# Eight copies of a pair's turned selection as one step on one engine, load issues planned at 1.4, and a new set of ranks

## The chip, the cores and the metric

The kernel runs on 1 core of one Trainium2 chip. The time is the device time of one execution in microseconds (us); "time before" is the median of 3 runs. Five engines work side by side, each through its own list of instructions in order: PE (matrix products), ACT (activation functions and copies), DVE (vector work), POOL (masks, casts and some DMA issues) and SP (most DMA issues).

## The reference: what is computed

Attention with a selection of key chunks comes first, for 4 batches of 8 heads with 768 positions of 64 values; a gated feed-forward layer over the 3072 tokens follows.

```python
k_min = np.min(k_chunks, axis=3)          # chunks of 32 keys, 24 chunks
k_max = np.max(k_chunks, axis=3)
ub = np.sum(np.maximum(q * k_min, q * k_max), axis=-1)   # a bound per query and chunk
ub = np.where(causal, ub, -1e9)
top_chunks = np.argsort(ub, axis=-1)[..., -6:]           # each query keeps 6 chunks
scores = np.where(sel & causal_by_position, scale * (q @ k.T), -1e9)
attn = softmax(scores); attn_out = attn @ v
x = attn_out as 3072 tokens x 512;  xn = x / rms * rms_g
out = (silu(xn @ w_gate) * (xn @ w_val)) @ w_out         # 512 -> 1536 -> 512
```

## The kernel before, in words

**Units of work.** The heads are taken in pairs: 16 pairs, four to a batch. For each pair `prep` (L465) loads q and k (step names `qload`, `kload`, L491, on SP), turns them by PE (`qT`, `kT`, L501), copies them out of PSUM (`qE`, `kE`), reduces the chunks to minima and maxima (`kmn`, `kmx`, DVE), computes the bounds on PE (`ub`, L588), copies and turns them (`ubE`, `up`), finds the sixth largest (`max`, L629) and writes the selection into a tile `selq` (`sel`, L636 and L640). PE turns that (`selT`, L651) into a PSUM tile `st`, and eight copies of 32 x 192 elements (`selC`, L661, executed in the helper `evict` at L295 on ACT and L299 on DVE) bring it into the rows of the query tile `qs` that add the selection to the scores. One copy goes with each of the two heads (`hl`) and each of four quarters of the queries (`g`). `scores` (L694) then multiplies (`sc`, L719), exponentiates (`exp`, ACT, L736, tile `pt`), for batches 1 to 3 masks the diagonal on POOL (`mask`, L742), multiplies by v (`av`, L755) and divides (`xb`, DVE, L770 and L771). Pair 3 alone is done in two halves of the queries (`PARTS`, L243), so it has the places `s3.0` and `s3.3`; all others go whole.

**The feed-forward layer.** When all four pairs of a batch are done, `norm` (L783) scales the rows, half a batch at a time (`sq`, `eps`, `root`, `xs`; a turn by PE for batch 0, by DMA for the others), and `ffn` (L863) runs 12 blocks of `gate` (L883, four matmuls of 384 columns), `tanh` (ACT, L890), `tg` (DVE, L896), `val` (L904) and `hh` (DVE, L912), and then three output tiles of twelve matmuls (`po`, L924), each copied (`poE`) and stored (`out`, L939). 48 idle-time matmuls (`busy`, L342, rank 1000 and more) on zeros run when PE has nothing else at the start.

**What sets the order.** Nothing waits for a scheduler on the chip. All steps are added to a planner (`Order`, L79), which plays through time with a cost for each step and engine, and emits the instructions in the order in which its steps start. An engine that is free in the plan takes the ready step with the smallest rank (L126 to L154); where a step has costs for two engines, the first one to be free with nothing of smaller rank takes it. A rank is the place of the pair or half batch (`TIMES`: `a` for prep, `l` for loads, `s` for scores, `n` for norm, `f` for the feed-forward layer, `w` for weights) plus the number of the step's kind for batch 0 or the later batches (`RANK`), plus a pace. The planner also hands out the buffers: the 8 PSUM banks are shared by all kinds of tile (`ps=8`, L233), a bank going to the next tile when the plan says that its last user is done. In the program the real waits for buffers and data then hold whatever the plan assumed.

The plan's costs of a copy of n elements are `0.065 + n * 0.00083` on ACT (L281) and `0.07 + n * 0.00104` on DVE (L284). The steps around the change are:

```python
ld = [add(w + "load", "SP", 1.1, rank(lr, b, w + "load"), load, opens=[nat[w]], load=n * 550)] * 2
fin.append(add("selC", "", {"DVE": dve(nq / 2), "ACT": act(nq)},
               rank(at, b, "selC", hl, "step"), sel_out, [sT], opens=[c.set], uses=[st]))
need = list(c.sel) + c_qz + ...      # every sc step waits in the plan for all steps of c.sel
```

Here `nq` is 192, so the plan counts 0.224 us for a copy on ACT and 0.170 on DVE, and takes the eight for independent of each other.

Of the kernel before, what the change touches and what calls it, by code (L numbers as in the profile page):

```python
# [11 lines left out]
ACT = mybir.ActivationFunctionType  # L12
# [12 lines left out]

RANK = (
    dict(
        av=68.81, dif=27.84, eps=227.72, exp=-53.17, kC=174.37, kE=-146.3, kT=-410.53,
        kload=-41.08, kmn=-9.51, kmx=106.52, max=-184.96, qC=69.13, qE=207.98, qT=-151.24,
        qload=-40.04, relu=-83.35, root=-346.12, sc=-47.1, sel=-150.06, selC=272.89,  # L30
        selT=-45.75, sq=136.63, tp=-15.96, tpE=-44.6, ub=-307.31, ubE=23.65, ubm=-192.71,
        up=-160.23, vload=-327.49, xb=278.11, xs=-341.07,
    ),
    dict(
        av=-40.18, dif=78.51, eps=-121.68, exp=5.8, gate=-52.28, hh=-172.1, kC=-37.64,
        kE=163.43, kT=-18.13, kload=69.85, kmn=172.23, kmx=-38.93, mask=-59.31, max=121.45,
        out=-40.26, po=26.47, poE=28.63, qC=177.4, qE=15.98, qT=16.85, qload=40.35, relu=1.22,
        root=-157.61, sc=-29.47, sel=120.96, selC=24.49, selT=-332.65, sq=322.32, tanh=156.94,
        tg=27.97, ub=-2.65, ubE=-289.61, ubm=194.29, up=17.47, val=-42.44, vload=48.52,
        xT=-304.79, xb=-39.13, xs=-25.77,  # L40
    ),
)

TIMES = {
# [15 lines left out]
}  # L60


# [139 lines left out]
def kernel(  # L202
# [13 lines left out]
    B, H, S, D = q.shape  # L216
    assert (P, D) == (128, 64) and S == 768
    CH = 32
# [10 lines left out]
    G = 4  # L229
# [22 lines left out]
    def add(name, engs, occ, rank, *a, **kw):  # L252
        return order.add(name, engs, occ, rank if isinstance(rank, dict) else {"": rank}, *a, **kw)

    def rank(place, b, kind, n=0, pace=None):
        r = {place: 1.0, f"{kind}.{min(b, 1)}": 1.0}
        if n:
            r[pace] = float(n)
        return r
# [14 lines left out]
    def tile_of(b, shape, dtype, name):  # L274
        pool = ps if b.kind == "ps" else sb
        b.tile = pool.tile(shape, dtype, name=name, tag=f"{b.kind}{b.slot}")
        return b.tile


    def act(n):  # L280
        return 0.065 + n * 0.00083  # L281

    def dve(n):
        return 0.07 + n * 0.00104  # L284
# [42 lines left out]
    def make_ident(e):  # L327
# [7 lines left out]
        out=first[:], in_=ident_f[:, 0:1], func=ACT.Exp), [c_id])  # L335
# [69 lines left out]
    def make_tri(e):  # L405
# [10 lines left out]
        out=gains[:], in_=moe_rms_g.rearrange("(o n) -> o n", o=1).to_broadcast([P, DM])),  # L416
        load=140000)
# [14 lines left out]
    for part in range(2):  # L432
# [6 lines left out]
                load=1000000) for part in range(2)]  # L439
# [7 lines left out]
    def make_pair(p):  # L447
        c = Pair()
        c.p, (c.b, c.pr) = p, divmod(p, NP)
        c.h0 = 2 * c.pr  # L450
        c.set, c.ku, c.v = Buf("set"), Buf("ku"), Buf("vext")
        c.ke, c.dif = {}, {}
        return c
# [11 lines left out]
    def prep(c, i0, nb, at, lr):  # L465

        p, b, h0 = c.p, c.b, c.h0
# [3 lines left out]
        nat, big = {}, {}  # L471
        done = {}
        for w, src in (("k", k), ("q", q)):
            nat[w], big[w] = Buf("nat"), Buf("qt")

            def load(e, w=w, src=src, r0=0, rn=nb):
                if nat[w].tile is None:
                    tile_of(nat[w], [P, NT, 2, D], FP32, w + "nat")
                t = nat[w].tile
                for hl in range(2):  # L480
                    eng = nc.scalar if p == 0 and hl else nc.sync
                    eng.dma_start(out=t[:, r0:r0 + rn, hl, :],
                                  in_=src[b, h0 + hl, (i0 + r0) * P:(i0 + r0 + rn) * P].rearrange(
                                      "(t p) d -> p t d", p=P))

            if p == 0:
                ld = [add(w + "load", "SP", 0.2, -200 + 2 * (w == "q") + r0 / 3,
                          lambda e, load=load, r0=r0: load(e, r0=r0, rn=3), opens=[nat[w]],
                          load=3 * P * 550) for r0 in range(0, nb, 3)]
            else:  # L490
                ld = [add(w + "load", "SP", 1.1, rank(lr, b, w + "load"), load, opens=[nat[w]],  # L491
                          load=n * 550)] * 2

            evs = []
            for j0 in range(0, nb, 3):
                bank = Buf("ps", "prep")

                def turn(e, w=w, j0=j0, bank=bank):
                    t = tile_of(bank, [P, 3 * P], FP32, "p" + w)
                    for j in range(3):  # L500
                        nc.tensor.transpose(  # L501
                            t[:, j * P:(j + 1) * P],
                            nat[w].tile[:, j0 + j].rearrange("p h d -> p (h d)"), ident_f[:])

                tr = add(w + "T", "PE", 0.33, rank(at, b, w + "T", j0, "step"), turn, [ld[j0 // 3], c_id],
                         opens=[bank], uses=[nat[w]])

                def out_(e, w=w, j0=j0, bank=bank):
                    if big[w].tile is None:
                        tile_of(big[w], [P, S], FP32, w + "t")  # L510
                    evict(e, big[w].tile[:, j0 * P:(j0 + 3) * P], bank.tile[:])

                evs.append(add(w + "E", "", {"ACT": act(384), "DVE": dve(384)},
                               rank(at, b, w + "E", j0, "step"), out_, [tr],
                               opens=[big[w]], uses=[bank]))
            done[w] = evs
# [16 lines left out]
        step = 3 if p == 0 else nb  # L533
        for x0 in range(0, nb, step):
# [7 lines left out]
                    uses=[big["k"]])]  # L542

        def diff(e):
# [5 lines left out]
                 uses=[mx, c.ku], port=True)  # L550
# [4 lines left out]
        for w, dst in (("k", KE), ("q", QS)):  # L555
            for hl in range(2):
                rows = slice(hl * D, (hl + 1) * D)

                def cast(e, w=w, dst=dst, hl=hl, rows=rows):
# [4 lines left out]
                                 uses=[big[w]]))  # L564
# [4 lines left out]
        def relu(e):  # L569
# [5 lines left out]
                 uses=[big["q"]], port=True)  # L575


        nq = n // G
        ub = [Buf("ps", "prep") for _ in range(2)]
        ubs = Buf("ubs")  # L580

        def bounds(e):
            t = [tile_of(x, [P, nq], FP32, "ub") for x in ub]
            for m, src in ((0, big["q"].tile), (1, rel.tile)):
                for g in range(G):
# [9 lines left out]
                 uses=[c.ku, big["q"], rel])  # L595
        ue = []
        for h in range(2):
            def ub_out(e, h=h):
                if ubs.tile is None:
# [5 lines left out]
                          uses=[ub[h]]))  # L605
        up, ubm, m8 = Buf("ps", "prep"), Buf("ubm"), Buf("small")
# [9 lines left out]
        def causal(e):  # L616
# [6 lines left out]
                   opens=[ubm], uses=[up])  # L623
# [8 lines left out]
        sq = Buf("selq")  # L632

        def pick(e):
# [10 lines left out]
                 opens=[sq], uses=[m8, ubm], port=True)  # L645
        st = Buf("ps", "prep")
# [6 lines left out]
                    ident_b[:])  # L653

        sT = add("selT", "PE", NU * 0.057, rank(at, b, "selT"), sel_turn, [pk, c_idb], opens=[st], uses=[sq])
        fin = []
        for hl in range(2):
            for g in range(G):
                def sel_out(e, hl=hl, g=g):
                    rows = slice((1 - hl) * D, (1 - hl) * D + CH)  # L660
                    evict(e, QS[c.set.slot][hl][rows, g * nq:(g + 1) * nq],  # L661
                          st.tile[g * CH:(g + 1) * CH, hl * nq:(hl + 1) * nq])

                fin.append(add("selC", "", {"DVE": dve(nq / 2), "ACT": act(nq)},
                               rank(at, b, "selC", hl, "step"), sel_out, [sT],
                               opens=[c.set], uses=[st]))
        c.sel = fin
        return fin

# [273 lines left out]
    for p in range(NPAIRS):  # L943
        c, b = make_pair(p), p // NP
# [42 lines left out]
```

## Time and profile before

| what | us |
|---|---|
| median of 3 runs (331.98 to 332.43) | 332.0 |
| the profiled execution's own time | 334.32 |
| its span, first to last instruction | 332.6 |
| PE busy in the span | 316.3 (95%) |
| DVE busy | 249.3 (75%) |
| ACT busy | 210.4 (63%) |
| POOL busy | 118.5 (36%) |
| granted TensorE clock, mean | 0.993 |

The profile is of one execution. An engine's busy time is the time in which it runs instructions of its own; a wait is the idle time just before an instruction, put down to the work that ended last before it. The ends of matmuls are modelled, so PE's busy time is an upper figure of its work. "PE gp L883 <- ACT qs L295" is to be read as: the matmul of line 883 that writes tile gp had to wait for the ACT instruction of line 295 that writes qs.

### The profile page before, as it was taken

What the parts mean: (1) busy time and instruction counts of PE and PEld (TensorE: products, weight loads), DVE (VectorE), ACT (ScalarE), POOL (GpSimd) and SP (SyncE); (2) the same over time, 40 slices, a digit from 0 to 9 for tenths busy, and PEclk for the clock granted to TensorE, in tenths of its full rate; (3) what the DMA queues carried; (4) which work ended last, traced back from release to release, by engine and by line L of the source; (5) the groups of instructions that cost most, each with busy time, mean ns of one, the idle gap of its engine ahead of it and who ended that gap; (6) DMA issues with size and microseconds to landing.
All of it is one profiled execution on the core that took longest, in us unless ns stands there. A gap on an engine that the chain in (4) does not pass through costs nothing.

```text
span 332.6 us, 8116 instructions
## 1 busy us (share of the span) xinstructions
PE 316.3 (95%) x3036; PEld 198.7 (60%) x3036; DVE 249.3 (75%) x698; ACT 210.4 (63%) x497; POOL 118.5 (36%) x176
## 2 busy tenths in 40 slices
PE   8999987999999999999799899999999999999995
PEld 4566664665568666655465566756666556546542
DVE  6879879898788888879897689866695968817600
ACT  4679988548859588865695783858848533324121
POOL 7837437330707677820276231822202200000000
PEclk9999999799999999999999999999999999999999
DMA  9999999998885495890025075110000150010013
GB/s 176 211 219 190 205 176 176 157 137 103 114 79 70 28 189 111 162 199 2 1 65 74 5 45 111 50 65 2 34 0 2 48 140 4 0 65 32 0 74 118
DMA packets 92503, 30.28 MB, mean 91 GB/s; under 512 B 85424, under 2 KB 89264, under 8 KB 92464
## 3 DMA queue, kind: packets, MB, share of 16 engines
q1 hardware_dynamic: 62352, 21.50, 29.1%
q0 software_dynamic: 28512, 7.87, 24.5%
q10 hardware_dynamic: 1600, 0.39, 0.6%
q8 instruction: 24, 0.39, 0.5%
q14 instruction: 15, 0.12, 0.1%
HBM read 28.57 MB, written 6.29 MB: 105 GB/s over the span
## 4 chain that ended last, share of the span: by engine, by line
PE 73%; ACT 15%; DVE 8%; issue 3%; ACTq 0%; DVEq 0%
PE po L924 17%; PE gp L883 15%; PE vp L904 15%; PE sc L719 8%; ACT pt L736 6%; PE av L755 5%; ACT qs L295 4%; PE busy L342 4%; PE ub L588 3%; PE pq L501 3%; PE pk L501 3%; DVE qs L299 2%; DVE tg L896 2%; DVE hh L912 2%; ACT junk L798 1%
## 5 line engine op out<-in xcount | busy, mean ns | idle before, releaser
L736 ACT ACTIVATE pt<-sc 128x512 bf16<-128x512 f32 (+3 forms) x192 | 89.4, 601 | 2.5 <-PE sc L719 2.3
L890 ACT ACTIVATE sg<-gp 128x384 bf16<-128x384 f32 x96 | 47.0, 496 | 56.4 <-PE gp L883 54.8
L883 PE MATMUL gp<-xT,wg 128*128 128x384 bf16 x384 | 77.7, 329 | 4.0 <-ACT qs L295 2.9
L904 PE MATMUL vp<-xT,wv 128*128 128x384 bf16 x384 | 78.1, 328 | 0.3 <-ACT qs L295 0.3
L924 PE MATMUL po<-wo,hh 128*128 128x512 bf16 x288 | 69.7, 379 | 0.0
L896 DVE SCALAR_TENSOR_TENSOR tg<-sg,gp 128x384 bf16<-128x384 bf16 x96 | 52.0, 549 | 16.8 <-ACT sg L890 14.9
L912 DVE TENSOR_TENSOR hh<-vp,tg 128x384 bf16<-128x384 f32 x96 | 52.5, 553 | 13.4 <-PE vp L904 10.1
L719 PE MATMUL sc<-qs,ke 128*128 128x128 bf16 (+5 forms) x420 | 55.4, 251 | 3.5 <-ACT qs L295 1.1
L883 PEld LDWEIGHTS <-wg 128*128 128x128 bf16 x384 | 37.2, 99 | 30.1 <-issue 5.6
L742 POOL TENSOR_SCALAR_AFFINE_SELECT pt<-pt 128x512 bf16<-128x512 bf16 (+1 forms) x48 | 25.9, 555 | 76.0 <-ACT pt L736 75.7
L904 PEld LDWEIGHTS <-wv 128*128 128x128 bf16 x384 | 36.6, 98 | 24.2 <-issue 1.7
L924 PEld LDWEIGHTS <-hh 128*128 128x128 bf16 x288 | 27.4, 98 | 27.3 <-issue 0.9
L719 PEld LDWEIGHTS <-ke 128*128 128x128 bf16 (+1 forms) x420 | 30.3, 97 | 15.4 <-issue 7.3
L755 PE MATMUL av<-vx,pt 128*128 128x65 bf16 x672 | 35.0, 194 | 1.6 <-ACT pt L736 1.2
L755 PEld LDWEIGHTS <-pt 128*128 128x128 bf16 x672 | 30.3, 98 | 10.1 <-ACT pt L736 3.1
L295 ACT ACTIVATE qs<-st 32x192 bf16<-32x192 bf16 x77 | 24.7, 321 | 16.1 <-DVE qs L299 12.3
L299 POOL CAST qs<-qt 64x768 bf16<-64x768 f32 x30 | 28.7, 957 | 16.6 <-ACT qt L295 9.3
L299 POOL CAST ke<-kt 64x768 bf16<-64x768 f32 x30 | 24.9, 831 | 24.1 <-ACT kt L295 19.1
L297 ACT ACTIVATE osb<-po 128x512 f32<-128x512 f32 x22 | 13.2, 600 | 24.0 <-PE po L924 23.9
L299 DVE COPY qs<-st 32x192 bf16<-32x192 bf16 x51 | 12.8, 252 | 12.2 <-ACT qs L295 10.6
L771 DVE TENSOR_TENSOR xb<-av,rden 128x384 bf16<-128x384 f32 (+1 forms) x34 | 18.2, 534 | 1.2
L629 DVE MAX8 m<-ubm 128x8 f32<-128x24 f32 x192 | 18.6, 168 | 0.3
(72 smaller groups left out, 337.5 us busy)
## 6 DMA issues: line engine op xcount, KB each, us to landing
out_dram<-osb SPq DMA_DIRECT2D x24, 256.0 KB, 2.2
knat<-in_k_dram SPq DMA_DIRECT2D x30, 192.0 KB, 4.7
qnat<-in_q_dram SPq DMA_DIRECT2D x30, 192.0 KB, 5.5
vx<-in_v_dram POOLq DMA_DIRECT2D x16, 192.0 KB, 6.3
wv<-in_moe_w_val_dram POOLq DMA_DIRECT2D x2, 768.0 KB, 8.2
wg<-in_moe_w_gate_dram POOLq DMA_DIRECT2D x2, 768.0 KB, 8.2
wo<-in_moe_w_out_dram POOLq DMA_DIRECT2D x2, 768.0 KB, 9.9
ke<-e_all SPq DMA_DIRECT2D x4, 96.0 KB, 3.6
```

Of the source, the lines that this page charges most:

```text
L295: nc.scalar.activation(out=out_, in_=in_, func=ACT.Copy)
L299: engine[e].tensor_copy(out_, in_)
L719: nc.tensor.matmul(t[:, x:x + m, :].rearrange("p a b -> p (a b)"), ke[kk, kb * P:(kb + 1) * P], qs[kk, q0 * P:(q0 + m) * P], start=not tri ...
L736: nc.scalar.activation(out=t[:, 0:nn, :], in_=sc.tile[:, 0:nn, :], func=ACT.Exp, scale=SCALE)
L742: nc.gpsimd.affine_select(out=pt.tile[:, 0:nd, :], in_=pt.tile[:, 0:nd, :], compare_op=ALU.is_ge, fill=0.0, base=0, pattern=[[0, nd], [1, ...
L755: nc.tensor.matmul(av.tile[:, qi - i0, :], pt.tile[:, x, :], VX[c.v.slot][:, hl * NT + kb, :], start=(begin and m == 0), stop=(left[0] == ...
L883: nc.tensor.matmul(t[:], wg[:, g, hs], XT[b].tile[:, g, cols], start=(g == 0), stop=(g == NP - 1))
L890: nc.scalar.activation(out=t[:], in_=gp.tile[:], func=ACT.Tanh, scale=0.5)
L896: nc.vector.scalar_tensor_tensor(out=t[:], in0=sg.tile[:], scalar=1.0, in1=gp.tile[:], op0=ALU.add, op1=ALU.mult)
L904: nc.tensor.matmul(t[:], wv[:, g, hs], XT[b].tile[:, g, cols], start=(g == 0), stop=(g == NP - 1))
L912: nc.vector.tensor_tensor(out=t[:], in0=vp.tile[:], in1=tg.tile[:], op=ALU.mult)
L924: nc.tensor.matmul(po.tile[:], hhs[ht].tile[:, th * P:(th + 1) * P], wo[:, ht, :], start=(ht == 0), stop=(ht == NHT - 1))
```

## The change

It has three parts. First, the eight `selC` steps become one: the planner gives all eight copies to one engine, in one piece, at eight times the old cost. The instructions themselves are the same. Second, the plan's cost of a load step on SP goes from 1.1 to 1.4. Third, all ranks and places are new. The lines with the numbers that the prediction uses are shown, and the code in full.

```diff
 RANK = (
     dict(
...
-        qload=-40.04, relu=-83.35, root=-346.12, sc=-47.1, sel=-150.06, selC=272.89,
+        qload=-32.34, relu=88.72, root=-18.52, sc=-288.27, sel=-74.91, selC=242.22,
...
-        up=-160.23, vload=-327.49, xb=278.11, xs=-341.07,
+        up=-50.53, vload=-452.21, xb=292.1, xs=-144.05,
...
-        root=-157.61, sc=-29.47, sel=120.96, selC=24.49, selT=-332.65, sq=322.32, tanh=156.94,
+        relu=169.65, root=-55.35, sc=-44.17, sel=63.94, selC=151.6, selT=-67.55, sq=441.97,
...
 TIMES = {
-    "a0": -60.58, "a1": 78.0, "a10": -34.94, "a11": 48.02, "a12": 323.37, "a13": 278.16, "a14":
+    "a0": -76.6, "a1": 300.86, "a10": -14.76, "a11": 46.9, "a12": 263.28, "a13": 268.28, "a14":
...
-    "pacef3.1": 12.3, "pacen": -1.98, "s0.0": -191.96, "s1.0": 69.35, "s10.0": 107.42, "s11.0":
-    202.62, "s12.0": 669.83, "s13.0": -133.06, "s14.0": 290.72, "s15.0": 449.52, "s2.0":
-    -121.26, "s3.0": -251.12, "s3.3": -59.64, "s4.0": 97.32, "s5.0": -118.31, "s6.0": -77.51,
-    "s7.0": 18.87, "s8.0": 60.45, "s9.0": 183.95, "step": -3.75, "w": -21.56, "w0": -65.19,
-    "w1": 9.3, "w2": 137.06, "w3": 64.97,
+    "pacen": -9.68, "s0.0": -217.42, "s1.0": 332.82, "s10.0": 141.85, "s11.0": 161.77, "s12.0":
+    622.37, "s13.0": -83.63, "s14.0": 333.95, "s15.0": 390.14, "s2.0": -253.87, "s3.0": -327.97,
+    "s3.3": 111.93, "s4.0": 145.18, "s5.0": -148.53, "s6.0": -163.48, "s7.0": -121.78, "s8.0":
+    41.16, "s9.0": -33.71, "step": 5.45, "w": -36.63, "w0": -35.71, "w1": 8.31, "w2": 349.33,
+    "w3": 170.92,
...
-                ld = [add(w + "load", "SP", 1.1, rank(lr, b, w + "load"), load, opens=[nat[w]],
+                ld = [add(w + "load", "SP", 1.4, rank(lr, b, w + "load"), load, opens=[nat[w]],
                           load=n * 550)] * 2
...
-        fin = []
-        for hl in range(2):
-            for g in range(G):
-                def sel_out(e, hl=hl, g=g):
-                    rows = slice((1 - hl) * D, (1 - hl) * D + CH)
+        def sel_out(e):
+            for hl in range(2):
+                rows = slice((1 - hl) * D, (1 - hl) * D + CH)
+                for g in range(G):
                     evict(e, QS[c.set.slot][hl][rows, g * nq:(g + 1) * nq],
                           st.tile[g * CH:(g + 1) * CH, hl * nq:(hl + 1) * nq])
 
-                fin.append(add("selC", "", {"DVE": dve(nq / 2), "ACT": act(nq)},
-                               rank(at, b, "selC", hl, "step"), sel_out, [sT],
-                               opens=[c.set], uses=[st]))
+        fin = [add("selC", "", {"DVE": 2 * G * dve(nq / 2), "ACT": 2 * G * act(nq)}, rank(at, b, "selC"),
+                   sel_out, [sT], opens=[c.set], uses=[st])]
         c.sel = fin
         return fin
```

More of the change, by code (lines that the diff above doesn't have):

```diff
@@ L27 @@
     dict(
-        av=68.81, dif=27.84, eps=227.72, exp=-53.17, kC=174.37, kE=-146.3, kT=-410.53,
-        kload=-41.08, kmn=-9.51, kmx=106.52, max=-184.96, qC=69.13, qE=207.98, qT=-151.24,
-        qload=-40.04, relu=-83.35, root=-346.12, sc=-47.1, sel=-150.06, selC=272.89,
-        selT=-45.75, sq=136.63, tp=-15.96, tpE=-44.6, ub=-307.31, ubE=23.65, ubm=-192.71,
-        up=-160.23, vload=-327.49, xb=278.11, xs=-341.07,
+        av=44.16, dif=-97.28, eps=234.4, exp=-39.86, kC=95.98, kE=-286.4, kT=-336.89,
+        kload=-73.52, kmn=-17.68, kmx=-34.4, max=-106.58, qC=151.39, qE=88.69, qT=-99.73,
+        qload=-32.34, relu=88.72, root=-18.52, sc=-288.27, sel=-74.91, selC=242.22,
+        selT=-133.48, sq=-121.77, tp=-99.44, tpE=-199.84, ub=-168.14, ubE=-83.95, ubm=-174.72,
+        up=-50.53, vload=-452.21, xb=292.1, xs=-144.05,
     ),
     dict(
-        av=-40.18, dif=78.51, eps=-121.68, exp=5.8, gate=-52.28, hh=-172.1, kC=-37.64,
-        kE=163.43, kT=-18.13, kload=69.85, kmn=172.23, kmx=-38.93, mask=-59.31, max=121.45,
-        out=-40.26, po=26.47, poE=28.63, qC=177.4, qE=15.98, qT=16.85, qload=40.35, relu=1.22,
-        root=-157.61, sc=-29.47, sel=120.96, selC=24.49, selT=-332.65, sq=322.32, tanh=156.94,
-        tg=27.97, ub=-2.65, ubE=-289.61, ubm=194.29, up=17.47, val=-42.44, vload=48.52,
-        xT=-304.79, xb=-39.13, xs=-25.77,
+        av=-201.89, dif=168.37, eps=-51.98, exp=99.7, gate=-72.93, hh=-103.97, kC=40.96,
+        kE=186.65, kT=-81.83, kload=43.24, kmn=363.56, kmx=-2.42, mask=-366.49, max=55.5,
+        out=-6.09, po=1.6, poE=186.83, qC=-84.42, qE=111.18, qT=-50.08, qload=18.72,
+        relu=169.65, root=-55.35, sc=-44.17, sel=63.94, selC=151.6, selT=-67.55, sq=441.97,
+        tanh=-17.83, tg=-53.98, ub=-8.44, ubE=-172.7, ubm=119.61, up=-67.54, val=-55.05,
+        vload=49.76, xT=-333.1, xb=-106.59, xs=-63.18,
     ),
```

18 rows, old and new, of the table TIMES are left out of this document.

## The prediction

> **What bounds the kernel now.** I read the page first, then busy time by stretches, then who waits for whom, then the engines' own timelines around those waits.
>
> The page gives the shares of the span, and PE and its clock in 40 slices of 8.3 us.
>
> ```profile
> span 332.6 us, 8116 instructions
> PE 316.3 (95%) x3036; PEld 198.7 (60%) x3036; DVE 249.3 (75%) x698; ACT 210.4 (63%) x497; POOL 118.5 (36%) x176
> PE   8999987999999999999799899999999999999995
> PEclk9999999799999999999999999999999999999999
> ```
>
> PE is idle for 332.6 - 316.3 = 16.3 us. The stretches (length, then busy us of PE, PEld, DVE, ACT, POOL, then PE's clock) say where:
>
> ```profile
> 0.00:19.40 19.40, 18.14 (x146) 10.65 (x147) 13.90 (x48) 10.56 (x19) 13.52 (x34) 1.00 1.17 190
> 19.40:40.00 20.60, 19.55 (x277) 14.14 (x276) 18.59 (x63) 19.53 (x52) 11.74 (x14) 1.00 1.35 210
> 40.00:58.00 18.00, 14.28 (x232) 10.27 (x231) 16.01 (x42) 16.23 (x42) 10.39 (x14) 1.00 1.01 178
> 58.00:66.00 8.00, 7.99 (x49) 4.93 (x49) 6.39 (x17) 4.16 (x9) 2.94 (x4) 0.79 0.97 168
> 66.00:160.00 94.00, 91.84 (x963) 60.17 (x961) 79.19 (x245) 67.12 (x166) 42.81 (x59) 1.00 0.77 106
> 160.00:188.00 28.00, 24.21 (x289) 15.31 (x288) 22.34 (x77) 19.45 (x49) 13.73 (x19) 1.00 0.24 42
> 188.00:240.00 52.00, 51.65 (x533) 33.61 (x531) 39.86 (x109) 38.12 (x91) 19.33 (x28) 1.00 0.28 49
> 240.00:300.00 60.00, 60.00 (x411) 34.84 (x408) 41.63 (x83) 26.72 (x58) 4.02 (x6) 1.00 0.13 36
> 300.00:333.00 33.00, 28.65 (x153) 14.74 (x151) 11.37 (x22) 8.48 (x16) 0.00 (x0) 0.98 0.15 56
> ```
>
> From 240 to 300 us PE never stops, so nothing in that stretch can be won by order. At the end 332.6 - 300 - 28.65 = 3.95 us pass after PE's last matmul, in a copy and a store that any order needs. What can move is before 240: 1.26 + 1.05 + 3.72 + 0.01 + 2.16 + 3.79 + 0.35 = 12.3 us of idle PE. Up to 58 us, before the first feed-forward matmul, DVE and ACT are as full as PE (from 19.4 to 40, 18.59 and 19.53 of 20.60). After it PE is the bound, and each microsecond in which it waits is one of the total.
>
> The waits put names to this:
>
> ```profile
> ACT qs L295 <- DVE qs L299: 12.3, 27, 1.7
> DVE qs L299 <- ACT qs L295: 10.6, 25, 0.9
> PE gp L883 <- ACT qs L295: 2.9, 3, 1.2
> PE sc L719 <- ACT qs L295: 1.1, 3, 0.4
> PE sc L719 <- DVE qs L299: 0.6, 1, 0.6
> PE vp L904 <- ACT qs L295: 0.3, 1, 0.3
> ```
>
> The copies of `selC` wait for each other, 22.9 us in sum, though they write different parts of `qs`. And PE waits 2.9 + 1.1 + 0.6 + 0.3 = 4.9 us for the last of them: `sc` because it reads `qs`, `gp` and `vp` because they take a PSUM bank, and the turned selection `st` holds one until its last copy. That is the largest named part of the 12.3 us. One pair shows it (start, length, wait before it in brackets):
>
> ```profile
> 162.72 0.77 DVE L299 COPY qs<-st 32x192 bf16<-32x192 bf16 x3
> 163.57 0.32 ACT L295 ACTIVATE qs<-st 32x192 bf16<-32x192 bf16 x1 [1.71 <-DVE qs L299]
> 163.93 0.25 DVE L299 COPY qs<-st 32x192 bf16<-32x192 bf16 x1 [0.45 <-ACT qs L295]
> 164.86 0.32 ACT L295 ACTIVATE qs<-st 32x192 bf16<-32x192 bf16 x1 [0.32 <-DVE qs L299]
> 165.23 0.81 PE L883 MATMUL gp<-xT,wg 128*128 128x384 bf16 x4 [1.06 <-ACT qs L295]
> ```
>
> The reader is to see a strict alternation: three copies on DVE, then ACT, DVE, ACT and so on, each starting when the other engine's ends. From 162.72 to 165.18 the eight take 2.46 us in a row, ACT stood still for 1.71 us before its first, and the gate starts 0.05 us after the last. The planner, which sees eight independent copies of 0.224 or 0.170 us, can finish them on two free engines in 1 / (1/0.224 + 1/0.170) x 8 = 0.77 us. So the plan gives the bank away about 1.7 us before the program can.
>
> **The change part by part.** *One step for the eight copies.* No instruction goes or comes. Their lengths:
>
> ```profile
> L295 ACT ACTIVATE qs<-st 32x192 bf16<-32x192 bf16 x77 | 24.7, 321 | 16.1 <-DVE qs L299 12.3 <-PE st L651 3.0 <-PE pk L501 0.3
> L299 DVE COPY qs<-st 32x192 bf16<-32x192 bf16 x51 | 12.8, 252 | 12.2 <-ACT qs L295 10.6 <-PE st L651 1.1
> 75.31 2.65 ACT L295 ACTIVATE qs<-st 32x192 bf16<-32x192 bf16 x8 [0.33 <-PE st L651]
> ```
>
> Eight on DVE take 8 x 0.252 = 2.02 us. Eight on ACT take 2.65 us, as the third row shows, for this kernel already has pairs whose copies all fell to ACT. So the chain of a pair is 0.44 us shorter than 2.46 on DVE and 0.19 us longer on ACT. More weighs that the plan now holds `st` and `sc` back for 8 x 0.170 = 1.36 us (DVE) or 1.79 us (ACT): its error falls from about 1.7 us to 0.66 (2.02 - 1.36) or 0.86 (2.65 - 1.79), by 0.84 at least. PE's timeline has eight such waits, these the first and the last:
>
> ```profile
> 37.29 0.90 PE L719 MATMUL sc<-qs,ke 128*128 128x512 bf16 x6 [0.42 <-ACT qs L295]
> 187.06 0.81 PE L883 MATMUL gp<-xT,wg 128*128 128x384 bf16 x4 [1.22 <-ACT qs L295]
> ```
>
> In order of time they are 0.42, 0.57, 0.42, 0.26, 0.21, 1.06, 0.64 and 1.22 us, together 4.80. With 0.84 us off each and none below zero, 0.22 and 0.38 are left of the two long ones: a gain of 4.2 us. Bounds: below, no gain, if all blocks go to ACT and the new order puts PE work as early behind them as now; above, all 4.8. I take 4.2, since behind the whole block at 75.31 to 77.96 PE has no wait in the list.
>
> The Trainium skill, page "TensorEngine Tiling (Array Packing)", section "PSUM Bottleneck", speaks against this edit: it advises to use both ScalarE and VectorE to empty PSUM. By that rule, with the row's 321 ns, four copies beside four would take 1.28 us and one engine would be slower by 0.7 to 1.4 us a pair. The trace does not agree here: the eight on two engines took 2.46 us, not half of 2.65.
>
> What is queued behind the block: on ACT the `exp` and `tanh` steps, for up to 2.65 us at a stretch, and behind those `av` and `tg`; on DVE `tg` and `hh`. After 58 us the other engine is free meanwhile, where now both stand in the alternation, so I count nothing. Before 58 us both are near full. A pair's copies average 77/16 x 0.321 = 1.54 us on ACT and 51/16 x 0.252 = 0.80 on DVE; in one piece one engine gets 1.1 (2.65 - 1.54) to 1.2 us (2.02 - 0.80) more, the other as much less. For four pairs that is 4.6 us on the fuller engine. From 40 to 58 PE idles 3.72 of 18.00, 0.21 us for each us that these engines need, so I charge 4.6 x 0.21 = 1.0 us; bounds 0 (the relief pays for it) and 4.6.
>
> *Longer load issues.* Nothing changes in the program but the order. A step issues two of these (ns min/median/max of one):
>
> ```profile
> L482 SPq DMA_DIRECT2D knat<-in_k_dram x32: 368/632/2167, 0.8 to 145.1; - x32
> L482 SPq DMA_DIRECT2D qnat<-in_q_dram x32: 367/660/2757, 1.9 to 141.2; - x32
> ```
>
> Two medians make 1.26 to 1.32 us, so 1.4 is nearer to the trace than 1.1. Thirty load steps are planned 0.3 us longer. No wait of PE in the list is put down to a load, so I count 0; bounds 0 and the 1.05 us of idle PE between 19.4 and 40, either way, as that is where loads are densest.
>
> *New ranks.* The sum of PE's work stays. In the ranks one shift stands out: pair 1. Its `sc` goes from 69.35 - 47.1 = 22 to 332.82 - 288.27 = 45, its `xb` from 347 to 332.82 + 292.1 = 625, its prep up by 223, while `sc` of pairs 5, 6 and 7 falls from -148, -107 and -11 to -193, -208 and -166. The issues of `wo` on POOL (w2, w3) go from 137 and 65 to 349 and 171:
>
> ```profile
> L428 POOL DMA_DIRECT2D wo<-in_moe_w_out_dram x2: 826/839/852, 71.0 to 83.7; - x2
> L924 PE MATMUL po<-wo,hh 128*128 128x512 bf16 x288 | 69.7, 379 | 0.0
> 110.85 0.86 PE po L924 x4
> ```
>
> They are issued at 71.0 and 83.7 and first used at 110.85, so there are 27 us of cover; gone, each us later costs PE one. For SP, `l1` moves up by 100 and passes no other load of the first batch. I count 0 for the ranks as a whole; the bounds are the cases below.
>
> Sum: 4.2 - 1.0 + 0 + 0 = 3.2 us faster. The profiled execution took 334.32 us, its span 332.6 and 1.7 us around it; it is 2.3 us over the median of 332.0. Differences carry over, so from the median 332.0 - 3.2 = 328.8 us. A measurement of this kernel tells about 0.2%, 0.66 us, from no change.
>
> **The rivals.** *The first feed-forward layer starts late (slower).* It waits for all of batch 0:
>
> ```profile
> 48.16 0.36 DVE L771 TENSOR_TENSOR xb<-av,rden 128x192 bf16<-128x192 f32 x1
> 53.44 0.36 DVE L771 TENSOR_TENSOR xb<-av,rden 128x192 bf16<-128x192 f32 x1
> 56.41 0.40 PE L849 MATMUL tp<-ident_b,xs 128*128 128x128 bf16 x4 [0.83 <-DVE xs L827]
> 58.01 2.40 PE L883 MATMUL gp<-xT,wg 128*128 128x384 bf16 x8 [0.73 <-ACT xT L295]
> 52.00:58.00 6.00, 3.90 (x65) 2.58 (x65) 5.97 (x13) 5.21 (x14) 4.62 (x6) 1.00 1.11 214
> 58.00:62.00 4.00, 3.99 (x15) 1.94 (x15) 2.39 (x10) 0.98 (x2) 0.87 (x1) 0.57 1.05 157
> ```
>
> Now pair 3 is last, in halves, so norm starts on the first half some 5 us before the second. With the new ranks pair 1 would be last, whole, and behind pairs of batch 1. If one such pair goes ahead, at 53.44/4 = 13.4 us a pair, with PE idle (6.00 - 3.90)/6.00 = 0.35 of the time as in that row, PE loses 4.7 us; a second sag of the clock like that of the last row adds (1 - 0.57) x 4 = 1.7. Against the gain of 3.2 this makes 332.0 - 3.2 + 6.4 = 335.2 us. It decides once the first gate is more than 3.2/0.35 = 9 us late, after 67 us. For it: the ranks. Against it: PE takes whatever is ready, and pair 1's loads still come before those of batch 1.
>
> The Trainium skill, "TensorE: Matmul & The Clock Gate", section "What's actually happening", has the clock halve only after an idle window of about 3.4 us; by that the second sag would be struck and this case 333.5 us. The trace does not agree: ahead of the 0.57 its longest PE wait is 0.83 us.
>
> *More than expected (faster).* All 4.8 us go, the 1.0 is not charged, and the stall before 58 is filled so that the sag of 1.7 goes as well: 332.0 - 6.5 = 325.5 us. For it: that sag followed waits of 0.83 and 0.73 us, small ones.
>
> *It doesn't do what it says.* All blocks go to ACT, the first engine that the planner asks, and the new order leans on them as hard as now: gain 0, 332.0 us. Against it: 51 of 128 copies went to DVE.
>
> *The two engines' share is lost.* With every block on ACT and PE waiting behind each, 16 x 0.19 = 3.0 us slower, 335.0. Against it: only eight waits of PE are named for 16 pairs. The section of the Trainium skill on the PSUM bottleneck, in "TensorEngine Tiling (Array Packing)", points to this side.
>
> **How the numbers follow.** The forecast 328.8 us, own range 326.8 (a gain of 4.8, plus 0.4 of loads) to 331.3 (the 0.66 that can be told): 0.40. More than that: 0.12. No difference: 0.08. Late feed-forward layer: 0.35. Lost share: 0.05. So faster 0.52, same 0.08, slower 0.40. The range goes from 325.5 to 336.8, which is 335.2 with half of the 3.2 not won; I leave 0.06 below and 0.10 above it.
>
> **What would show it.** Right: no waits of ACT and DVE `qs` for each other, eight copies in a row at 2.0 or 2.65 us, the PE waits for `qs` under 1 us in sum, the busy share before 58 us no lower, first gate before 60 us. Wrong: first gate after 67 us with idle PE and a clock below 1 before it; PE waits for `qs` still over 3 us; `po` waiting for `wo`; idle PE after 240 us.

## The result and the profile after

The changed kernel takes 328.13 us (median of 4 executions, 327.53 to 328.45) against 332.18 us before (331.98 to 332.43). The ratio is 0.9876 with a 95% interval of 0.9859 to 0.9893: 4.05 us faster, where 3.2 were forecast. The profiled execution took 328.23 us, its span 326.5. The two spans differ by 6.1 us and not by 4.05, because before's profiled execution, at 334.32, had a sag of the clock that most of its others had not.

The clock hides a part of the gain. Of 53 further executions of the kernel before, 39 had a mean granted clock of 0.997 or more and took 331.9 to 333.6 us; 14 had 0.992 to 0.994 and took 334.1 to 335.1. By their times, the four executions behind the 332.18 belong to the 39. The changed kernel's four had clocks of 0.988, 0.988, 0.988 and 0.995: each had a sag. The kernel after_bank_late further down, which differs from it in the choice of a bank alone, shows both: it took 326.2 to 326.4 us at a clock of 1.00 and 328.2 at 0.988. So at a like clock the new order is some 6 us ahead (332.2 - 326.2), and the sag takes about 2 of them back.

The page of the changed kernel, the same lines as before:

```profile
span 326.5 us, 8103 instructions
PE 313.2 (96%) x3036; PEld 198.3 (61%) x3036; DVE 242.8 (74%) x692; ACT 213.4 (65%) x505; POOL 114.1 (35%) x174
PE   8998987999999999989999999999999999999995
PEclk9999997899999999999999999999999999999999
```

And its stretches up to 188 us (length, then busy us of PE, PEld, DVE, ACT, POOL, and PE's clock):

```profile
0.00:19.40 19.40, 17.41 (x147) 9.82 (x148) 14.99 (x56) 11.37 (x22) 13.08 (x33) 1.00 1.22 186
19.40:40.00 20.60, 18.70 (x295) 14.49 (x295) 17.59 (x62) 18.99 (x49) 12.25 (x15) 1.00 1.31 203
40.00:58.00 18.00, 14.67 (x176) 9.45 (x174) 15.35 (x55) 13.25 (x30) 7.44 (x9) 0.84 1.13 202
58.00:66.00 8.00, 7.66 (x58) 4.74 (x57) 6.39 (x12) 5.38 (x15) 0.00 (x0) 0.93 1.01 94
66.00:160.00 94.00, 92.33 (x1023) 62.23 (x1021) 79.13 (x236) 74.52 (x188) 47.34 (x67) 1.00 0.72 117
160.00:188.00 28.00, 27.97 (x305) 19.39 (x303) 25.49 (x67) 22.46 (x54) 13.90 (x22) 1.00 0.12 10
```

The reader is to see one row: from 160 to 188 us PE now idles 28.00 - 27.97 = 0.03 us, where it idled 3.79 (28.00 - 24.21), and runs 305 matmuls instead of 289. Up to 58 us it idles more, 1.99 + 1.90 + 3.33 = 7.2 us against 6.0. In all, PE's idle time falls from 16.3 to 13.3 us. The two orders put different work at the same time, so a single stretch says less than the sum. The other 3.1 us of the span are in PE's busy time, though it is the same 3036 matmuls. A gate matmul is shown for 329 ns but follows the one before after 163 (0.65 us for four in the chain), so a wait of up to 0.17 us is covered by a modelled end. That the 3.1 us are such short waits is argued, not shown. The clock is not the reason, for it acts the other way: by the rows up to 188 us, PE ran at half clock for some 6.9 us after (0.84 of 18.00 and 0.93 of 8.00) and 3.4 before (0.79 of 8.00).

The copies by line and engine (busy us, mean ns, idle time before them and its causes):

```profile
L295 ACT ACTIVATE qs<-st 32x192 bf16<-32x192 bf16 x80 | 25.7, 321 | 4.0 <-PE st L651 2.6
L299 DVE COPY qs<-st 32x192 bf16<-32x192 bf16 x48 | 12.1, 253 | 4.5 <-PE st L651 3.7
```

Two pairs in the timeline, one of each engine:

```profile
34.35 2.12 DVE L299 COPY qs<-st 32x192 bf16<-32x192 bf16 x8
138.04 2.69 ACT L295 ACTIVATE qs<-st 32x192 bf16<-32x192 bf16 x8
```

And all waits of PE for them:

```profile
PE sc L717 <- ACT qs L295: 3.2, 5, 1.3
PE sc L717 <- DVE qs L299: 1.1, 2, 0.8
```

Ten pairs' copies run on ACT (80/8) and six on DVE, in one piece. Of the 22.9 us of ACT and DVE waiting for each other nothing is left. The gate and value matmuls, which waited 3.2 us for the bank of `st`, don't wait for it any more. But `sc`, which waits for the data, waits 4.3 us instead of 1.7. So all of PE's waits for `qs` fell by 0.6 us only, from 4.9 to 4.3. More was won elsewhere. These are three rows of before:

```profile
PE av L755 <- ACT pt L736: 1.2, 3, 0.9
PE st L651 <- DVE selq L640: 0.7, 2, 0.4
PE sc L719 <- DVE hh L912: 0.6, 2, 0.3
```

Of these 2.5 us one row is left:

```profile
PE av L753 <- ACT pt L734: 0.2, 1, 0.2
```

Some others grew, by 1.4 us in all (`gp` for `xT` from 0.7 to 1.0, for example). Of the 3.0 us of idle time that went, 0.6 are waits for `qs` and 2.4 are not.

### The profile page after: what moved, and what is told of

Same layout as the page of the kernel before. It is cut to its first block, busy times and chain, and to the rows that moved or that the text cites. A ratio compares the mean times of both kernels' runs of the same rounds, so it can differ in the third digit from the quotient of the medians.

```text
span 326.5 us, 8103 instructions
## 1 busy us (share of the span) xinstructions
PE 313.2 (96%) x3036; PEld 198.3 (61%) x3036; DVE 242.8 (74%) x692; ACT 213.4 (65%) x505; POOL 114.1 (35%) x174
## 4 chain that ended last, share of the span: by engine, by line
PE 86%; ACT 6%; DVE 4%; DMA 1%; issue 1%; ACTq 0%
PE gp L881 20%; PE vp L902 19%; PE po L922 18%; PE sc L717 10%; PE av L753 5%; ACT qs L295 4%; PE ub L588 4%; PE pq L501 3%; PE pk L501 2%; PE busy L342 2%; PE up L612 2%; DVE qs L299 1%; ACT pt L734 1%; DMA qnat<-in_q_dram 1%; PE st L651 1%
## 5 line engine op out<-in xcount | busy, mean ns | idle before, releaser
L888 ACT ACTIVATE sg<-gp 128x384 bf16<-128x384 f32 x96 | 47.8, 504 | 50.1 <-PE gp L881 47.3
L881 PE MATMUL gp<-xT,wg 128*128 128x384 bf16 x384 | 78.7, 333 | 1.0 <-DVE xT L299 1.0
L902 PE MATMUL vp<-xT,wv 128*128 128x384 bf16 x384 | 76.8, 328 | 0.0
L894 DVE SCALAR_TENSOR_TENSOR tg<-sg,gp 128x384 bf16<-128x384 bf16 x96 | 52.3, 551 | 28.7 <-ACT sg L888 27.3
L717 PE MATMUL sc<-qs,ke 128*128 128x128 bf16 (+5 forms) x420 | 53.4, 251 | 4.4 <-ACT qs L295 3.2
L740 POOL TENSOR_SCALAR_AFFINE_SELECT pt<-pt 128x512 bf16<-128x512 bf16 (+1 forms) x48 | 24.0, 518 | 78.3 <-ACT pt L734 78.2
L753 PEld LDWEIGHTS <-pt 128*128 128x128 bf16 x672 | 32.4, 98 | 11.0 <-ACT pt L734 1.8
L753 PE MATMUL av<-vx,pt 128*128 128x65 bf16 x672 | 38.4, 194 | 0.5 <-ACT pt L734 0.2
L299 POOL CAST qs<-qt 64x768 bf16<-64x768 f32 x30 | 27.3, 911 | 13.9 <-ACT qt L295 8.0
L295 ACT ACTIVATE qs<-st 32x192 bf16<-32x192 bf16 x80 | 25.7, 321 | 4.0 <-PE st L651 2.6
L825 DVE SCALAR_TENSOR_TENSOR xs<-xb,ri,gains 128x512 bf16<-128x512 bf16 x24 | 17.5, 767 | 2.4 <-DMA xT<-xs 2.0
```

The lines of the kernel that those rows point to most:

```text
L295: nc.scalar.activation(out=out_, in_=in_, func=ACT.Copy)
L299: engine[e].tensor_copy(out_, in_)
L717: nc.tensor.matmul(t[:, x:x + m, :].rearrange("p a b -> p (a b)"), ke[kk, kb * P:(kb + 1) * P], qs[kk, q0 * P:(q0 + m) * P], start=not tri ...
L740: nc.gpsimd.affine_select(out=pt.tile[:, 0:nd, :], in_=pt.tile[:, 0:nd, :], compare_op=ALU.is_ge, fill=0.0, base=0, pattern=[[0, nd], [1, ...
L753: nc.tensor.matmul(av.tile[:, qi - i0, :], pt.tile[:, x, :], VX[c.v.slot][:, hl * NT + kb, :], start=(begin and m == 0), stop=(left[0] == ...
L881: nc.tensor.matmul(t[:], wg[:, g, hs], XT[b].tile[:, g, cols], start=(g == 0), stop=(g == NP - 1))
```

## The experiments

Two theories stood at first. **A**: the alternation of the copies between two engines is the cost. **O**: the new order is the cause, whatever the copies do. Two more came with the first results. **P**: the plan hands on the bank of `st` before the copies are really done, and PE work is put there. **E**: what counts is only which engines stand in the copies.

The grouped step and the new ranks could not be tried apart. With the old ranks the planner finds no order for the grouped step, and with the new ranks none for eight steps: it comes to a point at which no step that is ready can get its buffers. So most kernels here keep an order and change one thing in it.

**The old order, all copies on one engine.**

```diff
     for s in done:
-        s.emit(s.eng)
+        s.emit("DVE" if s.name == "selC" else s.eng)    # the second kernel: "ACT"
```

> The kernel before in its own order, but every one of the 128 selC copies is issued on DVE; nothing else moves. Theory A (the alternation between two engines is the cost): a pair's copies run without handing over, about 2.1 us in a row; PE's waits for qs fall from 4.9 us to under 2, most of all the three gate waits between 160 and 190 us (1.06, 0.64, 1.22); the time falls from 332.2 to 328.5 to 330. Theory O (the new order is the cause, not the copies): the time stays within 0.7 us of 332.2 or rises, because DVE gets 77 x 0.252 = 19 us more.

> The kernel before in its own order, with every selC copy issued on ACT. Theory A in the form that the handing over costs: ACT needs 8 x 0.33 = 2.65 us a pair against about 2.5 now, so PE's waits for qs stay at 3 to 5 us, and only DVE is freed; 331 to 332.5 us. Theory O: within 0.7 us of 332.2 as well, or slower, since ACT gets 51 x 0.32 = 16 us more. If this is as fast as the DVE version, the length of the chain isn't what counts, but that two engines stand in it.

All on DVE took 339.55 us, ratio 1.0189 (1.0143 to 1.0235); all on ACT 335.09, ratio 1.0055 (1.0030 to 1.0080). Both are slower. PE's waits for `qs`, in the DVE version and then in the ACT version:

```profile
PE gp L883 <- DVE qs L299: 3.4, 4, 1.8
PE sc L719 <- DVE qs L299: 3.2, 5, 1.1
```

```profile
PE gp L883 <- ACT qs L295: 2.8, 4, 0.9
PE sc L719 <- ACT qs L295: 2.4, 4, 0.7
```

There is no alternation left, and the gates wait for the bank as before (3.4 and 2.8 against 2.9 us). Theory A falls in its plain form: one engine alone gains nothing in an order that was not made for it. Neither time lies in the range that theory A had for it.

**The new order, copies shared by two engines.**

```diff
-                    evict(e, QS[c.set.slot][hl][rows, g * nq:(g + 1) * nq],
+                    evict(("DVE", "ACT")[g % 2], QS[c.set.slot][hl][rows, g * nq:(g + 1) * nq],
```

The second kernel has `("ACT", "DVE")[hl]` in that place.

> The changed kernel in its own order, but the eight copies of a pair are issued by turns on DVE and ACT. Theory A: the waits of ACT and DVE for each other come back (20 us and more in sum), each pair ties up both engines for about 2.4 us, and the time rises from 328.1 to 330 to 332. Theory O: the time stays within 0.7 us of 328.1.

> The changed kernel in its own order, with the four copies of head 0 on ACT and the four of head 1 on DVE. The two heads write different tiles and read the same PSUM bank. If the copies wait for each other because of the tile that they write, the two fours run side by side, 1.3 us a pair, and the time falls to 326.5 to 327.8. If they wait because of the bank that they read, the fours run one after the other, 1.32 + 1.03 us and one hand-over, 2.4 us a pair, and the time is within 1 us of 328.1.

By turns: 352.10 us, ratio 1.0543 (1.0465 to 1.0621). By head: 339.47, ratio 1.0186 (1.0129 to 1.0243). One pair of the kernel by head, ACT and DVE:

```profile
94.56 1.32 ACT L295 ACTIVATE qs<-st 32x192 bf16<-32x192 bf16 x4
95.91 1.05 DVE L299 COPY qs<-st 32x192 bf16<-32x192 bf16 x4 [1.44 <-ACT qs L295]
```

DVE stood idle for 1.44 us and began 0.03 us after ACT's last copy, though its four write another tile. So it isn't the tile written that makes them wait. The hand-over itself is cheap (1.32 + 0.03 + 1.05 = 2.40 us, less than the 2.69 of eight on ACT); dear is that the second engine's list stops until the first one gets there: DVE waited 19.4 us for ACT in 15 such waits. Theory O is out: with its engines shared again the new order is 11 to 24 us slower. That goes for shared engines in an order that was planned for one; it is the mirror of the runs before it, and says that neither the copies nor the order will do alone. I had expected 2 to 4 us more for the turns and within 1 us for the split by head, both far too little.

**The old order, copied through SBUF.** This takes away what the copies have in common, the bank.

```diff
-        fin = []
+        fin, mid = [], []
...
                 def sel_out(e, hl=hl, g=g):
+                    if not mid:
+                        mid.append(sb.tile([P, NU * P], BF16, name="mid", tag=f"mid{p % 3}"))
+                        evict(e, mid[0][:], st.tile[:])
...
-                          st.tile[g * CH:(g + 1) * CH, hl * nq:(hl + 1) * nq])
+                          mid[0][g * CH:(g + 1) * CH, hl * nq:(hl + 1) * nq])
```

> The kernel before in its own order, with the copies on the engines that they had, but the turned selection is first copied whole from its PSUM bank to SBUF (128 x 384, about 0.5 us on the engine of the first copy, 16 more instructions), and the eight copies read that. If the copies wait for each other because they read one PSUM bank, these waits (22.9 us) go, the bank is free after 0.5 us, the three gate waits between 160 and 190 us (2.9 us) go too, and the loss of that stretch falls; 328.5 to 331 us in spite of 8 us more copying. If they wait because of the tile qs, the waits stay near 20 us and the time is 332 to 335.

332.73 us, ratio 1.0005 (0.9982 to 1.0028): no change in the time, where 328.5 to 331 had been expected, but much in the trace. The pair that the prediction showed at 162.72 us, here:

```profile
163.84 0.34 DVE L299 COPY mid<-st 128x384 bf16<-128x384 bf16 x1
164.22 1.10 DVE L299 COPY qs<-mid 32x192 bf16<-32x192 bf16 x5
164.21 1.10 ACT L295 ACTIVATE qs<-mid 32x192 bf16<-32x192 bf16 x3 [1.07 <-DVE mid L299]
165.12 0.81 PE L886 MATMUL gp<-xT,wg 128*128 128x384 bf16 x4
```

Two stretches of it:

```profile
58.00:160.00 102.00, 95.72 (x991) 63.70 (x999) 87.64 (x259) 75.00 (x180) 46.39 (x63) 1.00 0.78 114
160.00:188.00 28.00, 26.07 (x304) 16.57 (x306) 24.18 (x87) 22.41 (x55) 14.72 (x20) 1.00 0.24 42
```

Both engines start within 0.01 us of each other and run side by side, five copies beside three: 1.48 us from the first copy to the last instead of 2.46. None of the eight waits for one of the eight on the other engine any more (what is left is 2.7 + 2.1 us for the copy into SBUF), and the gate at 165.12 doesn't wait. So it was the common PSUM bank. From 160 to 188 PE idles 1.93 us instead of 3.79. From 58 to 160 us it idles 6.3 instead of 2.2: what was won is given back. PE waits there for DVE's `tg` (1.6 + 0.8 us), `qs` (1.2) and `selq` (1.1). That the 16 extra copies (10 on ACT of 531 ns, 6 on DVE of 352) make these late is likely, but not shown.

**The choice of the bank, with the order kept.** When a tile opens, the planner gives it the bank that has been free longest. These kernels count `st`'s bank as older or younger in that choice alone; the steps, their engines and their order stay as they are.

```diff
         st = Buf("ps", "prep")
+        st.sel = 1
...
-    key=lambda i: held[b.kind][i].done if held[b.kind][i] else -1.0)
+    key=lambda i: held[b.kind][i].done + (X if getattr(held[b.kind][i], 'sel', 0) else 0.0) if held[b.kind][i] else -1.0)
```

X is -50 in after_bank_soon and 1.9 in before_bank_late and after_bank_late.

> The changed kernel, step for step in the same order on every engine. Only the choice among the PSUM banks that are free in the plan differs: the next tile that opens takes the bank of the turned selection st first, if that is free in the plan, and not the bank that has been free longest. Theory P (the plan believes st's bank free before the copies are really done, and the loss is PE work put into it too early): PE's waits for qs rise from 4.3 us to 8 us or more and the time from 328.1 to 331 to 336. Theory E (what counts is which engines stand in the copies): engines and order are as before this edit, so the time stays within 0.7 us of 328.1.

> The kernel before, step for step in the same order, copies on the engines that they had. Only the choice of bank differs: the planner counts st's bank as 1.9 us younger than it is when it picks the bank that has been free longest. The three gates at 165.2, 181.9 and 187.1 us still get st's bank, since no other is free there; other tiles no longer do. Theory P: the waits of those three stay (2.9 us), those of other work for st's bank go; 331.3 to 332.3 us. Theory E: 332.0 to 332.6, no change.

> The changed kernel in the same order, with st's bank counted as 1.9 us younger in the choice of bank. Theory P: the waits of PE that came from the bank go, those for the data in qs stay; 327.3 to 328.1 us. Theory E: no change, 328.1 within 0.7.

On one chip the three took 329.55, 332.53 and 326.87 us, ratios 0.9909 (0.9886 to 0.9933), 1.0002 (0.9981 to 1.0023) and 0.9826 (0.9801 to 0.9852). PE's waits for `qs` in after_bank_soon, then in after_bank_late:

```profile
PE sc L718 <- ACT qs L295: 4.1, 6, 1.4
PE sc L718 <- DVE qs L299: 1.7, 2, 0.9
PE vp L903 <- ACT qs L295: 0.5, 1, 0.5
PE gp L882 <- ACT qs L295: 0.3, 1, 0.3
```

```profile
PE sc L718 <- ACT qs L295: 2.8, 3, 1.3
PE sc L718 <- DVE qs L299: 1.1, 2, 0.8
```

The same program order is 2.7 us slower when `st`'s bank is handed on at once, and its waits are 6.6 - 3.9 = 2.7 us longer. That the two agree is chance, for half of the 2.7 us is the clock: none of the six executions of after_bank_soon was above 0.994, while three of after_bank_late were at 1.00. At a like clock they are 328.79 and 328.83 us (0.994) against 327.38 and 327.48 (0.995), two executions each, so the choice of the bank is worth about 1.4 us. The direction is theory P's; the size is below the 331 to 336 us that it expected. Theory E had no change, and is out for the new order. before_bank_late came out at 332.53, as theory E had it, and not at theory P's 331.3 to 332.3: its gates still wait 2.9 us for `qs`, as they did. The reason given beforehand was that those three gates find no other bank free. after_bank_late doesn't differ from the changed kernel: 0.9826 and 0.9836 have overlapping intervals.

**The load part alone** is `"SP", 1.1` to `"SP", 1.4` in the kernel before.

> The kernel before with the second part of the change alone: the plan counts 1.4 for a load step in place of 1.1. The lists of instructions come out the same but for a handful that change places. Every theory has no change here, 332.2 within 0.7 us; a gain of 1 us or more would mean that the load part carries some of the 4.05 us.

331.86 us, ratio 0.9991 (0.9969 to 1.0013): no difference that can be told.

**Another order for the changed code.** All ranks were moved at random, with a standard deviation of 2 (`rank = rank + gauss(0, 2)` for each number but the paces).

> The changed code with every rank and place moved by a random amount (standard deviation 2). A plan comes out that uses the same steps in another order, and its own reckoning of the span is 1.3 us longer than that of the changed kernel. If the luck of an order is small beside the plan's reckoning, the time is 328 to 330 us. If orders that plan alike differ by several us on the chip, it lies outside 327 to 331, and then 4 us between two orders say little about the copies.

328.58 us, ratio 0.9870 (0.9837 to 0.9903). This order, too, is 3.9 us ahead of before, so the gain doesn't hang on one exact order. It is a near neighbour of the changed kernel's, though: ranks of up to some hundreds moved by about 2. One more order is all that was tried, and no newly searched order of the eight separate steps. The planner's own reckoning of the whole span speaks against a plan that is simply shorter: run on the two kernels, it gives 315.0 us before and 316.0 after, each by its own costs. The plan got longer and the program shorter.

**The clock.** In the profiled execution of the changed kernel it falls to half between 52 and 53 us, among PE's waits ahead of the first gate. Filling these waits:

```diff
-            def turn(e, xs=xs, tp=tp):
+            def turn(e, j=j, xs=xs, tp=tp):
                 t = tile_of(tp, [P, NP, P], BF16, "tp")
+                if half == 0:
+                    for _ in range(4 if j else 10):
+                        nc.tensor.transpose(t[:, 0, :], ident_b[:], ident_b[:])
                 for g in range(NP):
                     nc.tensor.transpose(t[:, g, :], xs.tile[:, g * P:(g + 1) * P], ident_b[:])
...
+                if b == 0 and c == 0 and hs.start == 0:
+                    for _ in range(6):
+                        nc.tensor.matmul(t[:], zeros[:, 0:P], zeros[:, 0:W], start=True, stop=True)
```

> The changed kernel once more, unchanged, so that it stands beside the next ones on one chip. Its executions so far show a mean granted clock of 0.988 with 328.0 to 328.5 us and of 0.995 with 327.5. If the clock is what makes the time vary, executions with a clock of 1.00 take about 326.2 us, those with 0.988 about 328.2, and nothing lies outside 326 to 328.5.

> The changed kernel in the same order, with extra PE work on zeros and on the identity where PE waits between 50 and 53.3 us: 10, 4 and 4 extra transposes into the tiles tp ahead of the first three turns of the normalised rows, and 6 extra matmuls of 384 columns ahead of the first gate, all overwritten by the real work. If the sag of the clock after 53 us comes from those idle stretches, the clock is 1.00 in every execution and the time 326.0 to 326.6 us. If the sag comes for another reason, clock and time vary as without it, 326.2 to 328.4 us.

The changed kernel again took 327.50 us (326.81 to 328.41), ratio 0.9836 (0.9807 to 0.9865), its clock always between 0.988 and 0.995. With the waits filled it took 325.83 (325.50 to 326.11), ratio 0.9785 (0.9759 to 0.9812), the best of all kernels here, with a clock of 0.998 to 1.000 each time. The two ranges of executions don't meet. The first gate of the changed kernel, and two stretches around it:

```profile
53.34 4.00 PE L881 MATMUL gp<-xT,wg 128*128 128x384 bf16 x12 [1.01 <-DVE xT L299]
```

```profile
50.00:54.00 4.00, 1.85 (x15) 1.02 (x16) 3.97 (x18) 2.53 (x6) 0.39 (x1) 0.78 1.15 204
54.00:59.00 5.00, 5.00 (x17) 2.29 (x16) 3.13 (x11) 1.47 (x3) 3.13 (x3) 0.50 1.17 210
```

The 3.41 us ahead of the fall, and a stretch of before_bank_late in which the clock didn't fall:

```profile
48.87:52.28 3.41, 2.08 (x27) 1.34 (x23) 3.29 (x10) 1.90 (x4) 1.52 (x2) 1.00 1.08 178
```

```profile
54.80:58.21 3.41, 1.69 (x15) 1.06 (x15) 3.41 (x13) 2.99 (x10) 3.11 (x4) 1.00 1.22 233
```

The first gate of the filled kernel, and the first two stretches there:

```profile
53.88 2.11 PE L887 MATMUL gp<-xT,wg 128*128 128x384 bf16 x12
```

```profile
50.00:54.00 4.00, 3.39 (x43) 2.44 (x42) 3.97 (x14) 2.40 (x6) 0.92 (x2) 1.00 1.16 203
54.00:59.00 5.00, 5.00 (x35) 3.08 (x34) 4.90 (x18) 2.60 (x7) 3.13 (x3) 1.00 1.16 208
```

Twelve gate matmuls take 4.00 us at half clock and 2.11 at full. The first gate is 0.54 us later with the filling, and the whole is 1.7 us faster (327.50 - 325.83).

## Why the prediction was right, point by point

- **The block of eight.** "I take 4.2" was the gain from PE's waits. The direction held, and so did the lengths of the blocks: 2.12 us on DVE for 2.02, 2.69 on ACT for 2.65. The part on the bank held: the 3.2 us of `gp` and `vp` went to 0, and after_bank_soon brings 0.8 us of them back by the choice of the bank alone. The part "with 0.84 us off each and none below zero" failed for the data: `sc`'s waits grew from 1.7 to 4.3 us, and the named waits for `qs` only fell from 4.9 to 4.3. So the term of 4.2 us is worth 0.6 in the waits that it was added up from. What it took for fixed was the work that stands behind a block: in the new order `sc` waits seven times for `qs`, where it waited four times. The sum came near by luck. Between the two profiled executions 2.4 us less of other idle time and 3.1 us less busy time come on top of the 0.6, which makes the 6.1; and some 2 of these are gone in the medians, since most executions of before had no sag and all of the changed kernel's had.
- **The signs.** Right were the copies in a row, no waits of ACT and DVE for each other, and a first gate before 60 us. Two came out on the other side: PE's waits for `qs` "under 1 us in sum" are 4.3, beyond the 3 that the prediction named as a sign of being wrong, and PE's busy time before 58 us went from 52.0 to 50.8 us, where it was to be no lower. Both speak against the first term as it was reckoned.
- **"Differences carry over."** The rows come from an execution of 334.32 us with a sag, the start of the sum from a median of 332.0. Going by the clocks of before's other executions, those at 332.0 had no such sag. At a like clock the gain is some 6 us, about twice the 3.2.
- **The alternation.** I named it as the thing to remove. before_all_dve and before_all_act show that its removal by itself loses time. What came with the gain is a plan that counts the copies in one piece on one engine, together with an order made for it; how much is due to either is open.
- **The charge of 1.0 us before 58 us** held as a number: 1.2 us more idle time there. The reason given did not: one of DVE and ACT was to get 4.6 us more to do, but up to 58 us both were busy for less, 47.9 and 43.6 us, where they had 48.5 and 46.3. What grew there is `sc`'s waits for `qs`, from 1.0 to 2.6 us.
- **Loads at 0** held: 0.9991, with the interval about 1, tried in the old order alone.
- **New ranks at 0; pair 1 late as the main rival (0.35).** This reading of the ranks was wrong. The first gate starts at 53.34 us, 4.7 us earlier than before, and not after 67. A rank only decides between steps that are ready, and from the ranks alone I could not tell which were. The earlier start didn't show as less idle time up to 58 us, and PE then ran at half clock.
- **More than expected (0.12)** had the sag of the clock go. It stayed in every execution of the changed kernel; with after_warm it was gone each time. That its 325.83 is close to the 325.5 given there is luck: the 325.5 takes 1.7 us for the sag off a median that, by the point above, had none, and takes all 4.8 us of waits for `qs` as gone.
- **The two engines' share.** The Trainium skill, "TensorEngine Tiling (Array Packing)", section "PSUM Bottleneck", advises both engines for emptying PSUM. For eight copies out of one bank this case disagrees: shared by head they ran one after the other in 2.40 us, and the kernel, in an order planned for one engine, took 339.47. Out of SBUF they did run side by side, 1.10 us beside 1.10.

Open stay the 3.1 us of PE's busy time, and what the grouped step is worth apart from the new ranks. A new search with the eight separate steps stands as an untested rival.

## What to carry to other kernels

Where an order is planned ahead, look for the step whose planned length and measured length differ most, and for the buffers that it holds: some of the loss sits with the work that the plan puts into those buffers too early (1.4 us here for the choice of one bank). Make the plan believe what the trace shows, then search anew, and judge by the chip, not by the length of the plan; one engine for the copies, forced into the old order, cost 1.8 to 6.3 us (0.55% and 1.89% of 332.5). Fill short waits of PE ahead of a dense stretch if the clock falls there.

## What the runs showed of the hardware

The clock fell to 0.50 at 52.3 us, although PE was busy for 2.08 of the 3.41 us ahead of that and none of its waits there was longer than 0.66 us. In before_bank_late PE was busy for 1.69 of 3.41 us, and the clock stayed at 1.00. So such a stretch can bring the sag and need not. With 3.39 of 4 us busy from 50 to 54 it stayed at 1.00, and the mean clock was 0.998 or more in all six executions. The Trainium skill, "TensorE: Matmul & The Clock Gate", section "What's actually happening", gives an idle window of about 3.4 us as the condition. Here a stretch of that length in which PE was busy for 2.08 of 3.41 us was enough.

Copies out of one PSUM bank on ACT and DVE waited for each other whatever they wrote (22.9 us in sum before, 1.44 us in the pair by head); the same copies out of one SBUF tile did not (1.10 us beside 1.10). The waits end with the other engine's semaphore, so they are the program's. The Trainium skill, "PSUM — Partial Sum Buffer", section "PSUM bank collisions raise a hardware error", explains why a program has them: two engines must not touch one bank in the same 32 partitions at once, and it allows other 32 partitions of the bank. The trace agrees on the bank and shows a coarser guard: each of the four quarters reads 32 partitions of its own, and DVE still waited until ACT had done all four. A guard by 32 partitions was not tried.
